# Reading the moving operands of two GEMMs in even, then odd 16-byte pieces

## The chip, the core and the metric

The kernel runs on one core of a Trainium2 chip. A core has TensorE (PE in the profile: matrix products, with weight loads listed as PEld), VectorE (DVE), ScalarE (ACT), GpSimd (POOL) and SyncE (SP), and 16 DMA engines. The metric is the device time of one launch in microseconds, lower is better. The median of three runs before the change is 673.26 us (673.08 to 673.38).

## The reference

Attention with a sliding window and four sink columns, followed by a two-layer network whose activation has a learned slope for negative values:

```python
keep = is_sink | in_window                     # 4 sinks, window of 128
scores = np.where(keep, q @ k.T / sqrt(64), -1e9)
a = softmax(scores);  attn = a @ v             # B, H, S, D = 4, 8, 768, 64
x = attn.transpose(0, 2, 1, 3).reshape(3072, 512)
h = x @ w_in                                   # 512 -> 2048
g = np.maximum(h, 0) + alpha * np.minimum(h, 0)
out = g @ w_out                                # 2048 -> 512
```

## The kernel before

The 3072 tokens are cut into 12 chunks of 256 (`QC`); a chunk lies within one batch entry. The hidden 2048 columns are cut into 16 blocks of 128, called f (`NF`). All weights are converted once, at the start, and stay in SBUF.

Products that need fp32 accuracy are made from parts in the type fp32r (four bytes, rounded, one pass of TensorE): a value is split into a high part and the rest, and three products are added: high x high, high x low and low x high. `xh` and `xl` are the parts of x, `gh` and `gl` those of g, and `fin` (called `w` in the profile) holds for one f the high and low parts of w_in and of w_out, 512 columns each.

For each chunk c and block f:

- `gemm1` (line 897) makes h for 128 hidden columns and 256 tokens. The stationary operand is 128x128 of w_in, the moving operand is 256 columns of `xh` or `xl`. There are four slices of the inner dimension (`KT`) and three products of each, so 12 matmuls of 256 columns, 2304 in all. Each has its own load of weights.
- ScalarE (L901, L903) and VectorE (L902, L904) make g, gh and gl from it.
- `gemm2` (L932, L934, L935; for the very last f of the last chunk L919 to L921) adds to the output of the chunk. The stationary operand is 128 tokens of gh or gl, the moving operand is the 512 columns of w_out's high or low part. These are six matmuls of 512 columns for each c and f, 1152 in all. It runs two f behind `gemm1` (`LAG`).

Both read the moving operand as one run of consecutive columns.

The attention of the next chunk is spread between these blocks: scores (L600, L601), softmax (L613, L617), weights times values (L789, L878, in plain fp32, 64 columns of the array at a time) and the sinks' part (L862). The end of a chunk's attention writes x: `av` for chunk 2 (L808, L811), `av_split` for chunks 0 and 1 (L844, L848), `av_four` for the others (L884, L885). Each time ScalarE writes the high part (a cast to fp32r) and VectorE the rest (a subtraction).

On L862, the moving operand is read in runs of 32 columns:

```python
nc.tensor.matmul(place(x), vt.at[:, x * P:(x + 1) * P],
                 st.at.rearrange("p (i u b) -> p u i b", u=2, i=4), start=x % 2 == 0, stop=False)
```

That makes eight runs of 32 columns (128 bytes) for 256. For the plain fp32 product of the heads' pairs 2 and 3, L878 reads its 256 moving columns in eight runs of 32 as well; L789 reads them in one run. VectorE writes runs of 32 columns on L773.

The order of instructions is not written by hand: `Plan` gives every operation a cost and draws a schedule, and each engine gets its instructions in that order. The planner's cost for a matmul is `mm(n)`, 0.456 ns a column. Short bf16 matmuls on a tile called `idle` (L1089, 512 columns) fill gaps in the first 44 us.

Behind all this stands a general version for other masks (`general`, `general_moe`). It runs only if a flag is set, which it is not with the inputs given.

On the host, w_in and w_out are laid out as one row of 512 values per partition and f; a DMA brings both for one f.

Of the kernel before, what the change touches and what calls it, by code (L numbers as in the profile page):

```python
# [19 lines left out]
P = 128  # L20
# [4 lines left out]
QC = 2 * P  # L25
# [264 lines left out]
def cast(n, psum=False):  # L290
    return (0.045 if psum else 0.092) + 0.84e-3 * n
# [27 lines left out]
ISSUE = 0.45  # L319
SINKLAG = 0.0  # L320
R_TAIL, N_TAIL, T_TAIL = 0.2, 0.65, 0.36


def program(ctx, tc, qk, pairs, vp, vq, vs, w, par, out):
# [474 lines left out]
    def av(c, p):  # L799
        src, v, bk = wt.pop((c, p)), vtile.pop((c, p)), val("pa")  # L800
        a = lambda: bk.at[:, :QC]
        vt, st = vst[c // CPB], sinkT[c]
        op("PE", mm(QC), lambda: nc.tensor.matmul(a(), vt.at[:, p * P:(p + 1) * P], st.at, start=True, stop=False),
           reads=[vt, st], writes=[bk], tail=R_TAIL)
        op("PE", values_cost(c), lambda: values(c, v.at, lambda j: src.at.bitcast(F32)[:, j * 4 * P:(j + 1) * 4 * P], a()),
           reads=[src, v], writes=[bk], tail=N_TAIL, mode="col")
        x1, x2 = begin_x(c, p)
        op("ACT", cast(QC, True), lambda: nc.scalar.copy(x1.at[:, p], a()), reads=[bk], writes=[(x1, p)])  # L808
        if p + 2 < KT:
            load_v(c, p + 2)  # L810
        op("DVE", dve(QC), lambda: nc.vector.tensor_tensor(x2.at[:, p], a(), x1.at[:, p].bitcast(F32), ALU.subtract),  # L811
           reads=[bk, (x1, p)], writes=[(x2, p)])

    def av_split(c, g):
        both = (2 * g, 2 * g + 1)
        src, v = [wt.pop((c, x)) for x in both], [vtile.pop((c, x)) for x in both]
        wide, rb = rinv[c, g], val("ob")
        rk = val("o" if c == 0 else "pa")

        def inverse():  # L820
            for n in range(2):
                for u in range(2):
                    nc.tensor.transpose(rk.at[:, (2 * n + u) * P:(2 * n + u + 1) * P],
                                        wide.at[:, (2 * u + n) * P:(2 * u + n + 1) * P], ident)
        op("PE", 4 * TURN, inverse, reads=[wide, known("ident")], writes=[rk], tail=T_TAIL)
        op("ACT", cast(4 * P, True), lambda: nc.scalar.copy(rb.at, rk.at), reads=[rk], writes=[rb])
        bk = val("pa")
        vt, st = vst[c // CPB], sinkT[c]

        def sinks():  # L830
            for n, x in enumerate(both):
                nc.tensor.matmul(bk.at[:, n * QC:(n + 1) * QC], vt.at[:, x * P:(x + 1) * P], st.at, start=n == 0, stop=False)
        op("PE", 2 * mm(QC), sinks, reads=[vt, st], writes=[bk], tail=R_TAIL)

        def both_values():
            for n in range(2):
                values(c, v[n].at, lambda j: src[n][j].at, bk.at[:, n * QC:(n + 1) * QC], n == 1)
        op("PE", 2 * values_cost(c), both_values, reads=[t for two in src for t in two] + v, writes=[bk], tail=N_TAIL, mode="col")
        x1, x2 = begin_x(c, 2 * g)
        op("DVE", dve(4 * P), lambda: nc.vector.tensor_tensor(rb.at, bk.at, rb.at, ALU.mult), reads=[bk], writes=[rb])  # L840
        view = lambda: rb.at.rearrange("p (n x) -> p n x", n=2)
        part = slice(2 * g, 2 * g + 2)
        keys = [(x1, x) for x in both], [(x2, x) for x in both]
        op("ACT", cast(4 * P), lambda: nc.scalar.copy(x1.at[:, part], view()), reads=[rb], writes=keys[0])  # L844
        if c and not g:
            for x in both:
                load_v(c, x + 2)
        op("DVE", dve(4 * P), lambda: nc.vector.tensor_tensor(x2.at[:, part], view(), x1.at[:, part].bitcast(F32), ALU.subtract),  # L848
           reads=[rb, *keys[0]], writes=keys[1])

    def av_four(c):
        every = range(KT)
        kept = [wt.pop((c, x)) for x in every]
        src = [*kept[:2], *kept[2], *kept[3]]
        v = [vtile.pop((c, x)) for x in every]
        bks = [val("pa") for _ in range(2)]
        vt, st = vst[c // CPB], sinkT[c]
        place = lambda x: bks[x // 2].at[:, x % 2 * QC:(x % 2 + 1) * QC]

        def sinks():  # L860
            for x in every:
                nc.tensor.matmul(place(x), vt.at[:, x * P:(x + 1) * P], st.at.rearrange("p (i u b) -> p u i b", u=2, i=4), start=x % 2 == 0, stop=False)  # L862
        op("PE", 4 * mm(QC), sinks, reads=[vt, st], writes=bks, tail=R_TAIL)
        x1, x2 = begin_x(c, 0)

        def all_values():
            for x in every:
                if x < 2:
                    values(c, v[x].at, lambda j: kept[x].at.bitcast(F32)[:, j * 4 * P:(j + 1) * 4 * P], place(x), x == 1)
                    continue  # L870
                t, e = kept[x]
                blocks = [(1, lambda j: t.at.rearrange("p (i j u b) -> p j u i b", i=4, j=2, u=2)[:, j], slice(0, 2 * P))]
                if c % CPB:
                    blocks.append((0, lambda j: e.at[:, j * QC:j * QC + P], slice(0, P)))
                blocks.append((2, lambda j: e.at[:, j * QC + P:(j + 1) * QC], slice(P, 2 * P)))
                for n, (blk, what, os) in enumerate(blocks):
                    for j in range(2):
                        nc.tensor.matmul(place(x)[j * D:(j + 1) * D, os], v[x].at[:, blk, j], what(j), start=False, stop=x == KT - 1 and n == len(blocks) - 1)  # L878
        op("PE", 4 * values_cost(c), all_values, reads=src + v, writes=bks, tail=N_TAIL, mode="col")
        for n, bk in enumerate(bks):  # L880
            part = slice(2 * n, 2 * n + 2)
            keys = [[(t, x) for x in range(2 * n, 2 * n + 2)] for t in (x1, x2)]
            view = lambda bk=bk: bk.at.rearrange("p (n x) -> p n x", n=2)
            op("ACT", cast(4 * P, True), lambda part=part, view=view: nc.scalar.copy(x1.at[:, part], view()), reads=[bk], writes=keys[0])  # L884
            op("DVE", dve(4 * P), lambda part=part, view=view: nc.vector.tensor_tensor(x2.at[:, part], view(), x1.at[:, part].bitcast(F32), ALU.subtract),  # L885
               reads=[bk, *keys[0]], writes=keys[1])

    gs = {}
# [1 line left out]
    def gemm1(c, f):  # L890
# [3 lines left out]
        def some(kt):  # L894
            ks = slice(kt * P, (kt + 1) * P)
            for n, (part, rhs) in enumerate(((0, x1), (0, x2), (1, x1))):
                nc.tensor.matmul(h(), fin.at[:, 0, part, ks], rhs.at[:, kt], start=(kt == 0 and n == 0), stop=(kt == KT - 1 and n == 2))  # L897
        for kt in range(KT):
            op("PE", 3 * mm(QC), lambda kt=kt: some(kt), reads=[fin, (x1, kt), (x2, kt)], writes=[bk], tail=R_TAIL)
        g, gh, gl = val("g"), val("gh"), val("gl")  # L900
# [8 lines left out]
    def gemm2(c, f, dst):  # L909
# [5 lines left out]
        if c == NCHUNK - 1 and f == NF - 1:  # L915
            for j in range(2):
                def last(j=j):
                    js = slice(j * P, (j + 1) * P)
                    nc.tensor.matmul(o2[j].at, gh.at[:, js], fin.at[:, 1, 0], start=False, stop=False)  # L919
                    nc.tensor.matmul(o2[j].at, gh.at[:, js], fin.at[:, 1, 1], start=False, stop=False)  # L920
                    nc.tensor.matmul(o2[j].at, gl.at[:, js], fin.at[:, 1, 0], start=False, stop=True)  # L921
                op("PE", 3 * mm(DM), last, reads=[fin, gh, gl], writes=[o2[j]], tail=R_TAIL)
                ob = val("ob")
                op("ACT", cast(DM, True), lambda ob=ob, j=j: nc.scalar.copy(ob.at, o2[j].at), reads=[o2[j]], writes=[ob])
# [2 lines left out]
        for lowpart in range(2):  # L927
            def some(lowpart=lowpart):
                for j in range(2):
                    js = slice(j * P, (j + 1) * P)  # L930
                    if lowpart:
                        nc.tensor.matmul(o2[j].at, gl.at[:, js], fin.at[:, 1, 0], start=False, stop=(f == NF - 1))  # L932
                    else:
                        nc.tensor.matmul(o2[j].at, gh.at[:, js], fin.at[:, 1, 0], start=(f == 0), stop=False)  # L934
                        nc.tensor.matmul(o2[j].at, gh.at[:, js], fin.at[:, 1, 1], start=False, stop=False)  # L935
            op("PE", (2 if lowpart else 4) * mm(DM), some, reads=[fin, gl if lowpart else gh], writes=o2, tail=R_TAIL)
        if f == NF - 1:
            for j in range(2):
# [184 lines left out]
def general_moe(nc, gen, ptile, f, x, wt, alt, acc):  # L1123
# [15 lines left out]
    nc.vector.tensor_tensor(gl, g, gh.bitcast(F32), ALU.subtract)  # L1139
    for j in range(2):  # L1140
        js = slice(j * P, (j + 1) * P)
        nc.tensor.matmul(acc[j], gh[:, js], wt[:, 1, 0], start=(f == 0), stop=False)
        nc.tensor.matmul(acc[j], gh[:, js], wt[:, 1, 1], start=False, stop=False)
        nc.tensor.matmul(acc[j], gl[:, js], wt[:, 1, 0], start=False, stop=(f == NF - 1))


def general_weights(nc, gen, src, dst):
# [133 lines left out]
```

## Time and profile before

| what | value |
|---|---|
| median of the runs | 673.26 us |
| the profiled execution, its own time | 673.32 us |
| its span, first to last instruction | 671.4 us |
| granted TensorE clock, mean | 0.999 |
| TensorE busy | 658.9 us, 4529 matmuls |
| weight loads busy | 577.5 us, 4529 loads |
| VectorE, ScalarE busy | 524.7 us, 397.2 us |

A row of the costliest groups reads: line, engine, operation, tile written <- tiles read, shape, count | busy time in us, mean ns of one | idle time of the engine before them and what ended it. Matmuls overlap in the pipeline, so the mean of one is longer than its share of the span. In the chain of waits a row has a start, a length and the work that filled it; `x12` are twelve instructions that follow each other. Rows by source line have the shortest, the median and the longest duration in ns.

### The profile page before, as it was taken

To read this page: it belongs to the slowest core of one execution; us is meant where nothing else is said; L and a number is where in the kernel's file an instruction comes from. 1 tells how busy PE (TensorE), PEld (TensorE's weight loads), DVE (VectorE), ACT (ScalarE), POOL (GpSimd) and SP (SyncE) were. 2 spreads that over 40 slices of the span, in tenths; PEclk is the share of its full clock that TensorE was granted. 3 is DMA by queue.
4 is the path that set the end of the run, shared out by engine and by line. 5 is a ranking of instruction groups with operands and counts; after the bars stand their busy time and mean duration, and the time that the engine had idled before them with its cause. 6 is when DMAs were issued, how large, how long until landed. Compare 5 with 4: busy or idle time off the path is not lost.

```text
span 671.4 us, 13234 instructions
## 1 busy us (share of the span) xinstructions
PE 658.9 (98%) x4529; PEld 577.5 (86%) x4529; DVE 524.7 (78%) x1750; ACT 397.2 (59%) x1066; POOL 34.5 (5%) x115
## 2 busy tenths in 40 slices
PE   8998999999999999999999999999999999999996
PEld 4577899978989989989989989988998988998985
DVE  7999999968958968976976986995995994994331
ACT  6999987737538537636736735745644753743332
POOL 2110000000000000000000000010000000000000
PEclk9999999999999999999999999999999999999999
DMA  8666542434434344443443443542542542420001
GB/s 326 217 248 236 185 165 59 116 87 147 132 103 143 114 124 123 133 140 87 144 122 101 143 127 96 160 120 73 167 133 70 163 138 80 143 95 17 32 2 35
DMA packets 58683, 84.67 MB, mean 126 GB/s; under 512 B 9072, under 2 KB 35056, under 8 KB 58608
## 3 DMA queue, kind: packets, MB, share of 16 engines
q1 hardware_dynamic: 55056, 70.64, 34.4%
q10 hardware_dynamic: 3552, 13.11, 5.4%
q8 instruction: 37, 0.61, 0.4%
q14 instruction: 38, 0.31, 0.1%
HBM read 66.69 MB, written 17.04 MB: 125 GB/s over the span
## 4 chain that ended last, share of the span: by engine, by line
PE 83%; DVE 11%; ACT 2%; issue 1%; POOL 0%; DMA 0%; ACTq 0%; DVEq 0%
PE bank L897 36%; PE bank L934 12%; PE bank L932 12%; PE bank L935 12%; PE bank L789 3%; PE bank L600 3%; PE bank L601 3%; PE bank L878 2%; DVE wa L398 2%; DVE w L406 2%; DVE wa L396 1%; DVE wa L389 1%; DVE pt L613 1%; ACT pt L617 1%; DVE gl L904 1%
## 5 line engine op out<-in xcount | busy, mean ns | idle before, releaser
L897 PE MATMUL bank<-xh,w 128*128 128x256 f32 x1536 | 306.5, 282 | 1.2 <-DVE g L902 1.2
L897 PEld LDWEIGHTS bank<-xh,w 128*128 128x128 f32 x1536 | 249.6, 189 | 9.9 <-DVE g L902 3.8
L897 PE MATMUL bank<-xl,w 128*128 128x256 f32 x768 | 214.3, 279 | 0.0
L901 ACT ACTIVATE g<-bank,param 128x256 f32<-128x256 f32 x192 | 90.6, 473 | 115.3 <-PE bank L897 110.8
L934 PE MATMUL bank<-w,gh 128*128 128x512 f32 x382 | 151.4, 396 | 0.5 <-ACT gh L903 0.5
L935 PE MATMUL bank<-w,gh 128*128 128x512 f32 x382 | 150.0, 393 | 0.0
L897 PEld LDWEIGHTS bank<-xl,w 128*128 128x128 f32 x768 | 144.5, 188 | 4.3
L617 ACT ACTIVATE pt<-pt,nm 128x260 f32<-128x260 f32 (+1 forms) x192 | 94.5, 493 | 50.7 <-DVE nm L613 50.4
L902 DVE TENSOR_TENSOR g<-bank,g 128x256 f32<-128x256 f32 x192 | 79.6, 419 | 51.8 <-ACT g L901 51.4
L932 PE MATMUL bank<-w,gl 128*128 128x512 f32 x382 | 119.7, 395 | 0.0
L903 ACT CAST gh<-g 128x256 fp32r<-128x256 f32 x192 | 76.9, 404 | 61.2 <-DVE g L902 61.1
L904 DVE TENSOR_TENSOR gl<-g,gh 128x256 fp32r<-128x256 f32 x192 | 80.2, 422 | 25.3 <-ACT gh L903 22.2
L613 DVE CUSTOM_DVE_ANT_0 pt<-bank,masks 128x260 f32<-128x260 f32 (+1 forms) x192 | 75.0, 401 | 14.9 <-PE bank L601 13.7
L932 PEld LDWEIGHTS bank<-w,gl 128*128 128x128 f32 x382 | 70.5, 188 | 16.1 <-issue 0.9
L934 PEld LDWEIGHTS bank<-w,gh 128*128 128x128 f32 x382 | 71.8, 188 | 9.1 <-ACT gh L903 0.8
L935 PEld LDWEIGHTS bank<-w,gh 128*128 128x128 f32 x382 | 71.8, 188 | 8.3
L566 DVE TENSOR_TENSOR kq<-stage,kq 64x392 fp32r<-64x392 f32 x80 | 45.2, 565 | 3.0 <-ACT kq L564 0.4
L662 POOL TENSOR_TENSOR sink<-pt,ri 128x8 f32<-128x8 f32 x80 | 19.8, 251 | 504.4 <-DVE ri L647 358.6
L601 PE MATMUL bank<-kq 128*128 128x260 f32 (+1 forms) x160 | 45.0, 281 | 0.0
L600 PE MATMUL bank<-kq 128*128 128x260 f32 (+1 forms) x160 | 44.7, 280 | 0.1
L658 DVE CUSTOM_DVE_ANT_0 comb<-pt,ri 128x128 f32<-128x128 f32 x136 | 43.1, 343 | 0.4
L564 ACT CAST kq<-stage 128x392 fp32r<-128x392 f32 x80 | 41.0, 512 | 2.5 <-PE bank L601 2.2
(131 smaller groups left out, 680.8 us busy)
## 6 DMA issues: line engine op xcount, KB each, us to landing
stage<-qk SPq DMA_DIRECT2D x80, 324.0 KB, 2.9
wraw<-w ACTq DMA_DIRECT2D x12, 1024.0 KB, 5.1
swap<-comb SPq DMA_DIRECT2D x36, 256.0 KB, 2.0
comb<-swap SPq DMA_DIRECT2D x36, 256.0 KB, 3.0
v<-vq SPq DMA_DIRECT2D x36, 192.0 KB, 2.5
out_dram<-ob SPq DMA_DIRECT2D x22, 256.0 KB, 3.5
wraw<-w SPq DMA_DIRECT2D x4, 1024.0 KB, 8.7
v<-vp SPq DMA_DIRECT2D x8, 192.0 KB, 8.1
```

Source lines behind the costliest of these rows:

```text
L600: nc.tensor.matmul(s[:, w0], qh()[:, qs], ks()[:, kw], start=True, stop=False)
L601: nc.tensor.matmul(s[:, w0], ql()[:, qs], ks()[:, kw], start=False, stop=True)
L613: op("DVE", dve(n), lambda: nc.vector.tensor_tensor_reduce(out=pt.at[:, u, w0], in0=s.at[:, w0], in1=masks[:, i, w0], scale=-0.125, scalar ...
L617: op("ACT", exp(n), lambda: nc.scalar.activation(pt.at[:, u, w0], pt.at[:, u, w0], AF.Exp, bias=nm.at[:, h, u:u + 1], scale=-1.0, accum_ou ...
L897: nc.tensor.matmul(h(), fin.at[:, 0, part, ks], rhs.at[:, kt], start=(kt == 0 and n == 0), stop=(kt == KT - 1 and n == 2))
L901: op("ACT", act(QC, True), lambda: nc.scalar.activation(g.at, h(), AF.Copy, scale=alt[:, f:f + 1]), reads=[bk, known("param")], writes=[g])
L902: op("DVE", dve(QC), lambda: nc.vector.tensor_tensor(g.at, h(), g.at, ALU.max), reads=[bk], writes=[g])
L903: op("ACT", cast(QC), lambda: nc.scalar.copy(gh.at, g.at), reads=[g], writes=[gh])
L904: op("DVE", dve(QC), lambda: nc.vector.tensor_tensor(gl.at, g.at, gh.at.bitcast(F32), ALU.subtract), reads=[g, gh], writes=[gl])
L932: nc.tensor.matmul(o2[j].at, gl.at[:, js], fin.at[:, 1, 0], start=False, stop=(f == NF - 1))
L934: nc.tensor.matmul(o2[j].at, gh.at[:, js], fin.at[:, 1, 0], start=(f == 0), stop=False)
L935: nc.tensor.matmul(o2[j].at, gh.at[:, js], fin.at[:, 1, 1], start=False, stop=False)
```

## The change

x and w_out are stored with their columns in another order. Take the pieces of four fp32 values (16 bytes) of a row in memory: the even pieces hold the first half of the columns, in order, and the odd pieces the second half. The matmuls of both GEMMs read their moving operand through a view that goes over all even pieces and then over all odd ones. So they take the columns in the same logical order as before, and outputs, stationary operands and sums are unchanged. For 256 columns these are 64 runs of four columns, for 512 they are 128.

x is written in that order by ScalarE and VectorE (their output, and the high part that the subtraction reads, go through the same view); w_out gets it on the host, before the launch. The general version reads w_out through the view too.

```diff
+def in_turn(a):
+    return a.rearrange("p (l t e) -> p t l e", t=2, e=4)
+def as_is(a):
+    return a.rearrange("p (t l e) -> p t l e", t=2, e=4)
...
 # av
-nc.scalar.copy(x1.at[:, p], a())
+nc.scalar.copy(in_turn(x1.at[:, p]), as_is(a()))
-nc.vector.tensor_tensor(x2.at[:, p], a(), x1.at[:, p].bitcast(F32), ALU.subtract)
+nc.vector.tensor_tensor(in_turn(x2.at[:, p]), as_is(a()), in_turn(x1.at[:, p].bitcast(F32)), ALU.subtract)
...
 # av_split; av_four in the same way, from the bank
-view = lambda: rb.at.rearrange("p (n x) -> p n x", n=2)
+view = lambda: rb.at.rearrange("p (n t l e) -> p t n l e", n=2, t=2, e=4)
+turned_ = lambda x: x.at[:, part].rearrange("p n (l t e) -> p t n l e", t=2, e=4)
-nc.scalar.copy(x1.at[:, part], view())
+nc.scalar.copy(turned_(x1), view())
-nc.vector.tensor_tensor(x2.at[:, part], view(), x1.at[:, part].bitcast(F32), ALU.subtract)
+nc.vector.tensor_tensor(turned_(x2), view(), turned_(x1).bitcast(F32), ALU.subtract)
...
 # gemm1
-nc.tensor.matmul(h(), fin.at[:, 0, part, ks], rhs.at[:, kt], ...)
+nc.tensor.matmul(h(), fin.at[:, 0, part, ks], in_turn(rhs.at[:, kt]), ...)
...
 # gemm2, all nine calls of the two GEMM2 forms and of general_moe
-nc.tensor.matmul(o2[j].at, gh.at[:, js], fin.at[:, 1, 0], ...)
+nc.tensor.matmul(o2[j].at, gh.at[:, js], in_turn(fin.at[:, 1, 0]), ...)
...
 # host
-w[:, 1] = inputs['moe_w_out'].reshape(NF, P, DM)
+w[:, 1] = inputs['moe_w_out'].reshape(NF, P, 2, DM // 8, 4).swapaxes(2, 3).reshape(NF, P, DM)
```

More of the change, by code (lines that the diff above doesn't have):

```diff
@@ L807, in av @@
         x1, x2 = begin_x(c, p)
-        op("ACT", cast(QC, True), lambda: nc.scalar.copy(x1.at[:, p], a()), reads=[bk], writes=[(x1, p)])
+        op("ACT", cast(QC, True), lambda: nc.scalar.copy(in_turn(x1.at[:, p]), as_is(a())), reads=[bk], writes=[(x1, p)])
         if p + 2 < KT:
             load_v(c, p + 2)
-        op("DVE", dve(QC), lambda: nc.vector.tensor_tensor(x2.at[:, p], a(), x1.at[:, p].bitcast(F32), ALU.subtract),
+        op("DVE", dve(QC), lambda: nc.vector.tensor_tensor(in_turn(x2.at[:, p]), as_is(a()), in_turn(x1.at[:, p].bitcast(F32)), ALU.subtract),
            reads=[bk, (x1, p)], writes=[(x2, p)])
@@ L840, in av_split @@
         op("DVE", dve(4 * P), lambda: nc.vector.tensor_tensor(rb.at, bk.at, rb.at, ALU.mult), reads=[bk], writes=[rb])
-        view = lambda: rb.at.rearrange("p (n x) -> p n x", n=2)
+        view = lambda: rb.at.rearrange("p (n t l e) -> p t n l e", n=2, t=2, e=4)
+        turned_ = lambda x: x.at[:, part].rearrange("p n (l t e) -> p t n l e", t=2, e=4)
         part = slice(2 * g, 2 * g + 2)
         keys = [(x1, x) for x in both], [(x2, x) for x in both]
-        op("ACT", cast(4 * P), lambda: nc.scalar.copy(x1.at[:, part], view()), reads=[rb], writes=keys[0])
+        op("ACT", cast(4 * P), lambda: nc.scalar.copy(turned_(x1), view()), reads=[rb], writes=keys[0])
         if c and not g:
@@ L847, in av_split @@
                 load_v(c, x + 2)
-        op("DVE", dve(4 * P), lambda: nc.vector.tensor_tensor(x2.at[:, part], view(), x1.at[:, part].bitcast(F32), ALU.subtract),
+        op("DVE", dve(4 * P), lambda: nc.vector.tensor_tensor(turned_(x2), view(), turned_(x1).bitcast(F32), ALU.subtract),
            reads=[rb, *keys[0]], writes=keys[1])
@@ L882, in av_four @@
             keys = [[(t, x) for x in range(2 * n, 2 * n + 2)] for t in (x1, x2)]
-            view = lambda bk=bk: bk.at.rearrange("p (n x) -> p n x", n=2)
-            op("ACT", cast(4 * P, True), lambda part=part, view=view: nc.scalar.copy(x1.at[:, part], view()), reads=[bk], writes=keys[0])
-            op("DVE", dve(4 * P), lambda part=part, view=view: nc.vector.tensor_tensor(x2.at[:, part], view(), x1.at[:, part].bitcast(F32), ALU.subtract),
+            view = lambda bk=bk: bk.at.rearrange("p (n t l e) -> p t n l e", n=2, t=2, e=4)
+            turned_ = lambda x, part=part: x.at[:, part].rearrange("p n (l t e) -> p t n l e", t=2, e=4)
+            op("ACT", cast(4 * P, True), lambda turned_=turned_, view=view: nc.scalar.copy(turned_(x1), view()), reads=[bk], writes=keys[0])
+            op("DVE", dve(4 * P), lambda turned_=turned_, view=view: nc.vector.tensor_tensor(turned_(x2), view(), turned_(x1).bitcast(F32), ALU.subtract),
                reads=[bk, *keys[0]], writes=keys[1])
@@ L896, in some @@
             for n, (part, rhs) in enumerate(((0, x1), (0, x2), (1, x1))):
-                nc.tensor.matmul(h(), fin.at[:, 0, part, ks], rhs.at[:, kt], start=(kt == 0 and n == 0), stop=(kt == KT - 1 and n == 2))
+                nc.tensor.matmul(h(), fin.at[:, 0, part, ks], in_turn(rhs.at[:, kt]), start=(kt == 0 and n == 0), stop=(kt == KT - 1 and n == 2))
         for kt in range(KT):
@@ L918, in last @@
                     js = slice(j * P, (j + 1) * P)
-                    nc.tensor.matmul(o2[j].at, gh.at[:, js], fin.at[:, 1, 0], start=False, stop=False)
-                    nc.tensor.matmul(o2[j].at, gh.at[:, js], fin.at[:, 1, 1], start=False, stop=False)
-                    nc.tensor.matmul(o2[j].at, gl.at[:, js], fin.at[:, 1, 0], start=False, stop=True)
+                    nc.tensor.matmul(o2[j].at, gh.at[:, js], in_turn(fin.at[:, 1, 0]), start=False, stop=False)
+                    nc.tensor.matmul(o2[j].at, gh.at[:, js], in_turn(fin.at[:, 1, 1]), start=False, stop=False)
+                    nc.tensor.matmul(o2[j].at, gl.at[:, js], in_turn(fin.at[:, 1, 0]), start=False, stop=True)
                 op("PE", 3 * mm(DM), last, reads=[fin, gh, gl], writes=[o2[j]], tail=R_TAIL)
@@ L931, in some @@
                     if lowpart:
-                        nc.tensor.matmul(o2[j].at, gl.at[:, js], fin.at[:, 1, 0], start=False, stop=(f == NF - 1))
+                        nc.tensor.matmul(o2[j].at, gl.at[:, js], in_turn(fin.at[:, 1, 0]), start=False, stop=(f == NF - 1))
                     else:
-                        nc.tensor.matmul(o2[j].at, gh.at[:, js], fin.at[:, 1, 0], start=(f == 0), stop=False)
-                        nc.tensor.matmul(o2[j].at, gh.at[:, js], fin.at[:, 1, 1], start=False, stop=False)
+                        nc.tensor.matmul(o2[j].at, gh.at[:, js], in_turn(fin.at[:, 1, 0]), start=(f == 0), stop=False)
+                        nc.tensor.matmul(o2[j].at, gh.at[:, js], in_turn(fin.at[:, 1, 1]), start=False, stop=False)
             op("PE", (2 if lowpart else 4) * mm(DM), some, reads=[fin, gl if lowpart else gh], writes=o2, tail=R_TAIL)
@@ L1141, in general_moe @@
         js = slice(j * P, (j + 1) * P)
-        nc.tensor.matmul(acc[j], gh[:, js], wt[:, 1, 0], start=(f == 0), stop=False)
-        nc.tensor.matmul(acc[j], gh[:, js], wt[:, 1, 1], start=False, stop=False)
-        nc.tensor.matmul(acc[j], gl[:, js], wt[:, 1, 0], start=False, stop=(f == NF - 1))
+        nc.tensor.matmul(acc[j], gh[:, js], in_turn(wt[:, 1, 0]), start=(f == 0), stop=False)
+        nc.tensor.matmul(acc[j], gh[:, js], in_turn(wt[:, 1, 1]), start=False, stop=False)
+        nc.tensor.matmul(acc[j], gl[:, js], in_turn(wt[:, 1, 0]), start=False, stop=(f == NF - 1))
 def general_weights(nc, gen, src, dst):
```

## The prediction, made before the changed kernel was run

> **What bounds the kernel now.** I read the page from the top: share of busy time, granted clock, the chain that ended last, then the costliest groups.
>
> ```profile
> span 671.4 us, 13234 instructions
> PE 658.9 (98%) x4529; PEld 577.5 (86%) x4529; DVE 524.7 (78%) x1750; ACT 397.2 (59%) x1066; POOL 34.5 (5%) x115
> PEclk9999999999999999999999999999999999999999
> PE 83%; DVE 11%; ACT 2%; issue 1%; POOL 0%; DMA 0%; ACTq 0%; DVEq 0%
> L897 PE MATMUL bank<-xh,w 128*128 128x256 f32 x1536 | 306.5, 282 | 1.2 <-DVE g L902 1.2
> L897 PE MATMUL bank<-xl,w 128*128 128x256 f32 x768 | 214.3, 279 | 0.0
> L934 PE MATMUL bank<-w,gh 128*128 128x512 f32 x382 | 151.4, 396 | 0.5 <-ACT gh L903 0.5
> L935 PE MATMUL bank<-w,gh 128*128 128x512 f32 x382 | 150.0, 393 | 0.0
> L932 PE MATMUL bank<-w,gl 128*128 128x512 f32 x382 | 119.7, 395 | 0.0
> ```
>
> TensorE works 98% of the span at its full clock, and nothing in the two GEMMs waits for another engine: the idle time before these groups is about a microsecond in all. What one matmul of them lasts is the kernel's time, one for one. The durations (282, 396 ns) overlap, since matmuls are pipelined; what counts is the distance from one start to the next. It comes from the chain of waits between 100 and 640 us, where that chain is TensorE's alone:
>
> ```profile
> by line: PE bank L897 42.3%; PE bank L934 14.0%; PE bank L932 13.9%; PE bank L935 13.9%; PE bank L789 3.7%; PE bank L600 3.5%; PE bank L601 3.4%; PE bank L878 2.7%; PE bank L862 0.8%; PE bank L731 0.3%; DVE w L406 0.2%; DVE wa L398 0.2%; PE
> ```
>
> That stretch has 1,967 matmuls on L897 and 983 on L932 to L935 (counts below). So one of 256 columns takes 0.423 x 540 us / 1967 = 116.1 ns of the chain, and one of 512 columns 0.418 x 540 / 983 = 229.6 ns. Groups of twelve on L897 in the same chain (start, length) are of two kinds:
>
> ```profile
> 263.82 1.36 PE bank L897 x12
> ...
> 267.06 1.41 PE bank L897 x12
> ...
> 273.08 1.42 PE bank L897 x12
> ...
> 279.64 1.36 PE bank L897 x12
> ```
>
> Same work, same shapes, 113.3 or 118 ns a matmul. The durations by line (shortest/median/longest, ns) show the same spread, and then what a matmul lasts while no weights are loaded:
>
> ```profile
> L897 PE MATMUL bank<-xh,w x1311: 276/280/388, 99.9 to 638.8; 128*128 128x256 f32 x188
> L897 PE MATMUL bank<-xl,w x656: 276/280/287, 99.8 to 638.7; 128*128 128x256 f32 x164
> L932 PE MATMUL bank<-w,gl x327: 388/392/505, 102.0 to 639.8; 128*128 128x512 f32 x164
> L934 PE MATMUL bank<-w,gh x328: 388/396/481, 101.1 to 639.4; 128*128 128x512 f32 x164
> L935 PE MATMUL bank<-w,gh x328: 388/393/403, 101.3 to 639.6; 128*128 128x512 f32 x164
> L932 PE MATMUL bank<-w,gl x1: 388/388/388, 549.7 to 549.7; 128*128 128x512 f32 x1
> 549.46 0.19 PEld L932 LDWEIGHTS bank<-w,gl 128*128 128x128 f32 x1
> 549.98 0.19 PEld L897 LDWEIGHTS bank<-xh,w 128*128 128x128 f32 x1 [0.32 <-DVE g L902]
> L1089 PE MATMUL bank<-idle x12: 379/379/382, 19.4 to 32.9; 128*128 128x512 bf16 x12
> ```
>
> The matmul that starts at 549.7 has no weight load beside it (the next starts at 549.98) and lasts the minimum, 388 ns. With one, 512 columns last up to 403 ns and 256 columns 276 to 287. So I read two losses: a variable one, when weight load and moving operand are read together (mean 394.4 - 388 = 6.4 ns on the three GEMM2 lines, 116.1 - 113.3 = 2.8 ns on L897), and a constant one, 388 against 379 ns for a bf16 matmul of the same width: 9 ns per 512 columns.
>
> **The change part by part.** Matmuls, weight loads, columns and bytes stay as they are; the 4529 records of each kind should return.
>
> 1. The reading order of the moving operand, in 2304 matmuls on L897 and 1152 on L919 to L935 (3 x 382 and 6). It is unpriced: no row reads in runs of four columns. The lowest bound by rows is that both losses go: 1152 x (6.4 + 9) + 2304 x (2.8 + 4.5) = 17.7 + 16.8 = 34.5 us less (4.5 is half of 9, an estimate). The highest comes from the one fp32r matmul with a broken reading order, the sinks' product on L862, in eight runs of 32 columns:
>
> ```profile
> L862 PE MATMUL bank<-sinkT,vs x36: 278/283/286, 186.4 to 605.9; 128*128 128x256 f32 x36
> L789 PE MATMUL bank<-wa,v 128*64 128x256 f32 x88 | 13.9, 394 | 0.0
> L878 PE MATMUL bank<-comb,v 128*64 128x256 f32 x72 | 10.8, 379 | 0.0
> ```
>
> Its median is 3 ns above L897's: 0.43 ns for each of seven joins between runs. Against that, the plain fp32 products show no price of a join: L878 reads eight runs of 32 and lasts 379 ns, L789 reads 256 in one run and lasts 394. [...] With 63 joins per 256 and 127 per 512 columns there are 291,456 joins; at 0.43 ns that is 125 us more.
>
> Between the two I take the variable loss as gone and the constant one as kept. The row nearest to the edit is L897's own: one address pattern, one shape, and yet whole groups lock into 1.36 or into 1.41 us. So the loss hangs on how two regular streams fall on each other, and the change alters just that: the moving stream keeps to even pieces for half its columns, while the load goes through all of them. After a first collision has shifted one against the other, I expect them to stay apart, as in the 1.36 us groups. Gain: 2304 x 2.8 = 6.4 and 1152 x 6.4 = 7.3, together 13.7 us.
>
> The Trainium skill speaks against this in "SBUF — State Buffer", section "Who interferes with whom": TensorE has two independent read ports, and it never waits on anyone. By that a load costs the matmul nothing and this term would be 0 us, the sum 673.3. The rows above (388 without a load, a mean of 394.4 with it) disagree, and I go by them.
>
> 2. Writing x in pieces: L884/L885, L844/L848, L808/L811.
>
> ```profile
> L884 ACT CAST xh<-bank 128x512 fp32r<-128x512 f32 x18 | 10.6, 587 | 25.0 <-PE bank L789 15.9 <-PE bank L878 9.0
> L885 DVE TENSOR_TENSOR xl<-bank,xh 128x512 fp32r<-128x512 f32 x18 | 12.5, 692 | 25.5 <-ACT xh L884 25.5
> L844 ACT CAST xh<-ob 128x512 fp32r<-128x512 f32 x4 | 2.4, 612 | 0.0
> L848 DVE TENSOR_TENSOR xl<-ob,xh 128x512 fp32r<-128x512 f32 x4 | 2.7, 683 | 0.0
> L773 DVE TENSOR_TENSOR wa<-comb,tri 128x256 f32<-128x256 f32 x72 | 27.2, 406 | 0.0
> L904 DVE TENSOR_TENSOR gl<-g,gh 128x256 fp32r<-128x256 f32 x192 | 80.2, 422 | 25.3 <-ACT gh L903 22.2 <-PE bank L1051 0.5
> 561.64 0.69 DVE L885 TENSOR_TENSOR xl<-bank,xh 128x512 fp32r<-128x512 f32 x1 [1.04 <-ACT xh L884]
> 565.50 0.28 PE L897 MATMUL bank<-xh,w 128*128 128x256 f32 x1
> ```
>
> L773 handles runs of 32 in 406 ns, L904 one run of 256 in 422: broken order costs VectorE nothing there. I take 0 us. If each of these took twice as long, the cover is the time from the last xl (ends 561.64 + 0.69 = 562.33) to its first use at 565.50: 3.2 us, against 2 x (0.59 + 0.69) = 2.6 us more. Uncovered is only the start, where chunks 0 and 1 feed TensorE directly: 2 x (0.612 + 0.683) = 2.6 us for one chunk's two pairs, the upper bound. Behind a longer L884 on ScalarE stand L901 and L903 of the next f; GEMM2 runs two f behind them.
>
> 3. w_out is permuted on the host. Its transfer stays one row of the same length, and the conversions (L384 to L406) work element by element: 0 us, either side, since no instruction, byte count or order of theirs changes.
>
> 4. `general_moe` doesn't run with these inputs (no row of its lines): 0 us.
>
> Sum: the profiled execution took 673.32 us (671.4 us of span and 1.9 around it), 0.06 from the median of 673.26. 673.3 - 13.7 = 659.6 us.
>
> **The rivals.**
>
> *Both losses go.* The constant 9 ns might also come from the order in which consecutive pieces are read. For it: it grows with fp32r and is absent in bf16, so it hangs on bytes per column. Against: it stands unmoved in every state, at 276 and 388. Price -34.5 us: 638.8 us.
>
> *Nothing moves.* The pieces are still whole ones, each read in four columns. The Trainium skill has such a rule ("SBUF — State Buffer", section "Specifications (TRN2)": lines of 16 bytes, a penalty for crossing to a new one); by it the crossings are equally many and the time stays. As a mechanism of this kernel: 64 and 128 pieces per matmul before and after, and the phases mix as now, half the groups at 1.36 and half at 1.41. 673.3 us. Against it: the chain's groups react to phase, so an exact tie needs a coincidence.
>
> *Slower by collisions.* While the moving stream stays on even pieces, every second piece of the load meets it on the same side, for the whole load; there is no phase to lock into. Then each matmul lasts its longest, 287 instead of 280 ns on L897 and 403 instead of 394.4 on GEMM2: 2304 x 7 + 1152 x 8.6 = 26 us, 699.3 us. It decides as soon as L897's mean start distance passes 116.1 ns. For it: L862, whose order is broken, never reaches 276 and lasts 283. Against: L862's longest, 286, stays within L897's.
>
> *Slower by joins.* Each join has a price of its own. At 0.43 ns: 673.3 + 125 = 798 us. From 0.047 ns a join (13.7 us / 291,456) on, the forecast's gain is eaten. For it: L862's shortest, 278, lies above 276. Against: L878.
>
> **How the numbers follow.** The forecast's case gets 0.34, both losses gone 0.13, nothing 0.12, collisions 0.24, joins 0.17. L862 is the sole near row for joins, and its 3 ns may be collisions as well, so joins stay below collisions. A change under 0.2% (1.3 us) can't be told from none in this kernel. Faster: 0.34 + 0.13 = 0.47; same 0.12; slower 0.24 + 0.17 = 0.41. The range runs from the second case (638.8, less 2.6 for its rounded terms) to the collisions' case with the uncovered x at the start and some joins (699.3 + 2.6 + 4): 636 to 706, which leaves the joins out. The likeliest case alone: 653 to 667, that is half to one and a half times its gain.
>
> **What would show it.** Right: the two kinds of groups on L897 become one at about 1.36 us; medians of 276 and 388 ns; L884 and L885 near 587 and 692 ns; TensorE still at 98%. Both losses gone: shortest durations under 276 and 388. Collisions: medians near 287 and 403, with a matmul that has no load beside it still at 388. Joins: that matmul longer too, by the same per column in all lines. Wrong altogether, if idle time appears before L897 with ACT xh or DVE xl as its releaser.

## The result and the profile after

The changed kernel takes 678.14 us (median of 4, 677.75 to 679.57) against 673.27 us: ratio 1.0076, 95% interval 1.0059 to 1.0094. It is slower by 4.9 us; 659.6 us was forecast. The profiled execution took 679.57 us, 1.4 above its median: in one slice of its page the clock was granted at 8 tenths, which the kernel before doesn't show there, so single times of it are read with 1 to 2 us in mind.

The page after, the same rows as before (L908 is the first GEMM, L943 to L946 the second):

```profile
span 677.6 us, 13234 instructions
...
PE 666.2 (98%) x4529; PEld 582.3 (86%) x4529; DVE 525.6 (78%) x1750; ACT 399.0 (59%) x1066; POOL 34.6 (5%) x115
...
PEclk9998999999999999999999999999999999999999
...
L908 PE MATMUL bank<-xh,w 128*128 128x256 f32 x1536 | 310.2, 283 | 1.1 <-DVE g L913 1.1
...
L908 PE MATMUL bank<-xl,w 128*128 128x256 f32 x768 | 215.5, 281 | 0.0
```

Count and shapes are the same, TensorE is as busy as before, and still next to nothing waits for another engine. Each matmul takes a little longer. In the chain of waits, the prediction read the groups of twelve on the first GEMM (start, length) as two kinds, 1.36 and 1.41 us. After, the stretch from 262 to 284 us has seven of them, 1.41 or 1.42 us each. Four of these:

```profile
263.32 1.41 PE bank L908 x12
266.61 1.41 PE bank L908 x12
269.88 1.41 PE bank L908 x12
272.93 1.42 PE bank L908 x12
```

They became nearly one kind, as the prediction's test asked, but the long one. From the starts of all whole groups between 100 and 640 us: after, 115 of 143 last 1.41 or 1.42 us and the others longer. Before, 63 of 144 lasted 1.36 to 1.39 us, 51 lasted 1.40 to 1.42, and 30 longer; there were more kinds than two. The durations by line (shortest/median/longest, ns), and last a wide matmul that has no weight load beside it:

```profile
L908 PE MATMUL bank<-xh,w x1299: 277/280/386, 99.8 to 639.2; 128*128 128x256 f32 x186
L943 PE MATMUL bank<-w,gl x324: 391/394/501, 101.2 to 637.6; 128*128 128x512 f32 x162
L945 PE MATMUL bank<-w,gh x326: 392/395/478, 100.2 to 639.8; 128*128 128x512 f32 x163
L946 PE MATMUL bank<-w,gh x326: 392/393/399, 100.5 to 640.0; 128*128 128x512 f32 x163
L943 PE MATMUL bank<-w,gl x1: 391/391/391, 554.8 to 554.8; 128*128 128x512 f32 x1
```

The weight loads around that last one (start, length):

```profile
554.34 0.42 PEld L943 LDWEIGHTS bank<-w,gl 128*128 128x128 f32 x2
555.07 0.19 PEld L908 LDWEIGHTS bank<-xh,w 128*128 128x128 f32 x1 [0.32 <-DVE g L913]
```

The shortest durations rose, 276 to 277 and 388 to 391 ns. The matmul without a load beside it (it starts at 554.8, the next load at 555.07) went from 388 to 391 as well, but one such matmul says little. Between 100 and 640 us each trace has eight wide ones with no load in their first 230 ns: before, six last 388 ns and two 392 and 393; after, five last 391 and three 394. The longest plain ones (403 on L935 before, 399 on L946) fell. So the floor went up and the spread went down.

How much it is: from the starts of matmuls that follow each other, leaving out those behind which TensorE waited (over 130 and 245 ns), the mean distance is 116.2 ns before and 117.9 after on the first GEMM (2238 and 2242 of them), 231.2 and 232.7 on the second (1125 each). 2304 x 1.8 + 1152 x 1.4 = 5.7 us (an estimate), and 4.9 were measured.

The writing of x shows no price (rows of ScalarE and VectorE after; 587 and 692 ns before). Only the four casts of chunks 0 and 1 went from 612 to 626 ns, 0.06 us in all.

```profile
L895 ACT CAST xh<-bank 128x512 fp32r<-128x512 f32 x18 | 10.6, 587 | 26.0 <-PE bank L798 17.0 <-PE bank L888 9.0
L896 DVE TENSOR_TENSOR xl<-bank,xh 128x512 fp32r<-128x512 f32 x18 | 12.5, 692 | 26.5 <-ACT xh L895 26.5
```

### The profile page after: what moved, and what is told of

Its sections match the earlier page's. It is cut to its first block, busy times and chain, and to the rows that moved or that the text cites. A ratio compares the mean times of both kernels' runs of the same rounds, so it can differ in the third digit from the quotient of the medians.

```text
span 677.6 us, 13234 instructions
## 1 busy us (share of the span) xinstructions
PE 666.2 (98%) x4529; PEld 582.3 (86%) x4529; DVE 525.6 (78%) x1750; ACT 399.0 (59%) x1066; POOL 34.6 (5%) x115
## 4 chain that ended last, share of the span: by engine, by line
PE 89%; DVE 7%; ACT 2%; issue 1%; POOL 0%; DMA 0%; ACTq 0%; DVEq 0%
PE bank L908 39%; PE bank L943 13%; PE bank L945 13%; PE bank L946 13%; PE bank L798 3%; PE bank L610 3%; PE bank L609 3%; PE bank L888 2%; DVE wa L407 1%; DVE w L415 1%; DVE wa L398 1%; DVE pt L622 1%; PE bank L872 1%; ACT pt L626 1%; ACT wa L393 0%
## 5 line engine op out<-in xcount | busy, mean ns | idle before, releaser
L908 PE MATMUL bank<-xh,w 128*128 128x256 f32 x1536 | 310.2, 283 | 1.1 <-DVE g L913 1.1
L908 PEld LDWEIGHTS bank<-xh,w 128*128 128x128 f32 x1536 | 249.9, 188 | 10.1 <-DVE g L913 3.6
L908 PE MATMUL bank<-xl,w 128*128 128x256 f32 x768 | 215.5, 281 | 0.0
L946 PE MATMUL bank<-w,gh 128*128 128x512 f32 x382 | 150.4, 394 | 0.0
L908 PEld LDWEIGHTS bank<-xl,w 128*128 128x128 f32 x768 | 144.4, 188 | 4.3
L943 PE MATMUL bank<-w,gl 128*128 128x512 f32 x382 | 120.4, 396 | 0.0
L943 PEld LDWEIGHTS bank<-w,gl 128*128 128x128 f32 x382 | 70.4, 188 | 16.5 <-issue 0.5
L946 PEld LDWEIGHTS bank<-w,gh 128*128 128x128 f32 x382 | 71.9, 188 | 8.6
```

The source lines that it names most:

```text
L908: nc.tensor.matmul(h(), fin.at[:, 0, part, ks], in_turn(rhs.at[:, kt]), start=(kt == 0 and n == 0), stop=(kt == KT - 1 and n == 2))
L943: nc.tensor.matmul(o2[j].at, gl.at[:, js], in_turn(fin.at[:, 1, 0]), start=False, stop=(f == NF - 1))
L946: nc.tensor.matmul(o2[j].at, gh.at[:, js], in_turn(fin.at[:, 1, 1]), start=False, stop=False)
```

## The experiments

Ratios are against the kernel before on the same chip.

**One GEMM at a time.** `e1` keeps the change for x alone, `e2` for w_out alone:

```diff
 # e1: gemm2, general_moe and the host layout as before; one line of each kind is shown
-nc.tensor.matmul(o2[j].at, gh.at[:, js], in_turn(fin.at[:, 1, 0]), ...)
+nc.tensor.matmul(o2[j].at, gh.at[:, js], fin.at[:, 1, 0], ...)
 # e2: gemm1 and the writing of x as before
-nc.tensor.matmul(h(), fin.at[:, 0, part, ks], in_turn(rhs.at[:, kt]), ...)
+nc.tensor.matmul(h(), fin.at[:, 0, part, ks], rhs.at[:, kt], ...)
```

> Only x is stored and read in even, then odd pieces; w_out is read as one run, as before. In the changed kernel's trace a 256-column matmul on the first GEMM starts 117.9 ns after the one before it, against 116.2 before, and without a weight load beside it lasts 278 instead of 276 ns. Theory A (the new reading order costs each matmul a constant amount of its own): 2304 x 1.8 = +4.1 us, ratio 1.006, and shortest durations of 278 ns on the first GEMM and 388 on the second. Theory B (the added time is collisions with weight loads, whose phase runs on from one GEMM to the other): the two halves don't add up; this one gives anything between -3 and +8 us, and the second GEMM's lines change as well.

> Only w_out is stored and read in even, then odd pieces; x as before. In the changed kernel's trace a 512-column matmul starts 232.7 ns after the one before, against 231.2, and without a load beside it lasts 391 instead of 388 ns. Theory A: 1152 x 1.4 = +1.6 us, ratio 1.0025, shortest duration of 391 ns on the second GEMM and 276 on the first. Theory B: not additive with the other half, between -3 and +5 us.

Measured: x alone 677.55 us, ratio 1.0062 (1.0049 to 1.0076); w_out alone 674.19 us, 1.0012 (1.0003 to 1.0021). The two add up to 1.0074; both together gave 1.0076. That speaks for A, though w_out alone stays below A's 1.0025. Most of the loss is x's. With w_out alone the first GEMM keeps its 276 ns and the second has the raised floor:

```profile
L906 PE MATMUL bank<-xh,w x1312: 276/278/388, 99.7 to 639.7; 128*128 128x256 f32 x188
L941 PE MATMUL bank<-w,gl x326: 391/394/501, 102.0 to 638.2; 128*128 128x512 f32 x163
```

A did not hit everything: in `e1`, the first GEMM starts every 117.9 ns as A said, but the second moved from 231.2 to 232.1 without an edit to it, and in `e2` the first fell from 116.2 to 115.7. So each GEMM's spacing also depends on the other's, which is what B said of the phase; the runs don't rule out that some of the added time is of that kind.

**The reading orders by themselves.** `e3` and `e5` add groups of equal matmuls behind the end of the kernel before, 32 or 40 in a row, with one line for each group:

```diff
+def turn(a, t, e):
+    return a.rearrange("p (l t e) -> p t l e", t=t, e=e)
 # M(o, n), W(o, n): n columns from column o of two converted weight tiles
 # one such line per order, width and load:
+plan.emit(lambda: [nc.tensor.matmul(hb[0:1, :256], W(0, 1), turn(M(16, 256), 2, 4), start=True, stop=True) for _ in range(32)])
```

> The kernel before with 1280 matmuls more behind its end, in groups of 32 that each repeat one reading order, with a stationary operand of 1 column (next to no load) or of 128. Their results are thrown away. Theory A: with 1 column, 256 columns in even-odd pieces last 2 ns more than in one run (278 against 276) and 512 columns 3 ns more; if it is a price of a join, it grows with the number of runs (4x4, 2x4, 2x8, 2x16, 2x32 have 64, 64, 32, 16 and 8 runs), if it is one jump a matmul, all orders cost alike. Theory B: with 1 column all orders with whole pieces last the same, and they differ only with 128. Where single columns are taken with a step of two or pieces of two columns (2x1, 2x2), each piece of memory is touched twice as often: up to double the time if a piece costs two steps. The two scans move the start of the moving operand by 16 bytes against the load's: if the variable loss (113.3 against 118 ns) is a collision of two regular streams, the start distances in them spread from 113 to 123 ns and from 226 to 240, the same for all 32 of a group but the first few; if the offset doesn't matter, all sixteen groups show one value for each width.

In `e3`, L1100 to L1107 have a load of 1 column, which takes 82 ns instead of 188 and so is little, but not none; their orders (t x e: turns by columns in a run) are one run, 2x4, 4x4, 2x8, 2x16, 2x32, 2x2 and 2x1. L1108 to L1110 have a load of 128 columns and the orders one run, 2x4 and 4x4. Loads and matmuls by duration, for the two loads and for the first three orders:

```profile
L1100 PEld LDWEIGHTS bank<-w,w x32: 81/82/83, 665.3 to 669.0; 128*1 128x1 f32 x32
L1100 PE MATMUL bank<-w,w x32: 276/276/280, 665.6 to 669.1; 128*1 128x256 f32 x32
L1101 PE MATMUL bank<-w,w x32: 277/279/280, 669.2 to 672.8; 128*1 128x256 f32 x32
L1102 PE MATMUL bank<-w,w x32: 270/271/277, 672.9 to 676.4; 128*1 128x256 f32 x32
L1108 PEld LDWEIGHTS bank<-w,w x32: 187/188/211, 702.5 to 706.3; 128*128 128x128 f32 x32
```

The chain of `e3` (start, length of 32 matmuls):

```profile
665.74 3.65 PE bank L1100 x32
669.38 3.72 PE bank L1101 x32
673.10 3.53 PE bank L1102 x32
676.63 3.70 PE bank L1103 x32
680.33 3.90 PE bank L1104 x32
684.22 3.78 PE bank L1105 x32
688.00 7.46 PE bank L1106 x32
695.47 7.47 PE bank L1107 x32
702.94 3.77 PE bank L1108 x32
706.70 3.84 PE bank L1109 x32
710.54 3.72 PE bank L1110 x32
```

Leaving out the first eight of each group, which still settle, the mean start distances with 1 column are 113.3 ns for one run, 116.3 for even-odd (2x4), 110.0 for 4x4, 115.6 for 2x8, 121.8 for 2x16 and 118.2 for 2x32. With 128 columns it is 117.8, 120.0 and 115.7 for the first three. All of these have one start of the moving operand against the load, 64 bytes on. Four things follow for it:

- The order of pieces has a price that needs no wide weight load: +3.0 ns for even-odd on 256 columns, and -3.3 ns for 4x4.
- It is not a price of joins: 4x4 has 64 runs, as many as 2x4, and is the shortest; 2x16 has 16 and is the longest of whole pieces.
- The wide load adds to these three orders: 4.5 ns to one run, 3.7 to even-odd, 5.7 to 4x4. Changing the moving order does not take it away.
- A piece read only by half (2x2, 2x1) costs double, 233 ns. The Trainium skill ("SBUF — State Buffer", section "Specifications (TRN2)") asks for two hits in a line of 16 bytes for full bandwidth; for these fp32r matmuls the runs show that two hits aren't enough.

For 512 columns, the groups don't settle the size: with 1 column 231.6 ns in one run and 230.7 even-odd, with 128 columns 233.2 and 233.5. A's 3 ns don't show there; the small price of `e2` is carried by the kernels alone.

In the two scans, one run of 256 columns settles at 113.35 ns when the moving operand starts 64 or 112 bytes after the load and between 116.7 and 120.0 otherwise; 512 columns range from 226.65 (start 0) to 233.4 (96). The spread lies inside the expected one, though not every group settles at one value. Two cautions follow. With the wide load, the start alone moves one run by 6.7 ns, and at two starts of eight no price of the load is left; the 2.2 ns between one run and even-odd lie inside that spread, so there the price of the order rests on the kernels. And L1108 has the relative start 64 as well but takes 117.8 ns: the scan's group differs from it in that both streams begin 96 bytes further on, and in what ran before it. The relative start alone doesn't set the value.

**More steps, and four turns in the kernel.** In `e4`, the changed kernel has t=4 instead of t=2, in the views and on the host:

```diff
-    return a.rearrange("p (l t e) -> p t l e", t=2, e=4)
+    return a.rearrange("p (l t e) -> p t l e", t=4, e=4)
...
-    w[:, 1] = inputs['moe_w_out'].reshape(NF, P, 2, DM // 8, 4).swapaxes(2, 3).reshape(NF, P, DM)
+    w[:, 1] = inputs['moe_w_out'].reshape(NF, P, 4, DM // 16, 4).swapaxes(2, 3).reshape(NF, P, DM)
```

> The changed kernel with four turns instead of two: every fourth piece of 16 bytes first, then those behind them, for x and w_out. Joins: as many as with two turns. In the groups of repeated matmuls, 256 columns in that order start 110.0 ns apart with a stationary operand of 1 column (113.3 in one run, 116.3 even-odd), and 115.7 with 128 columns (117.8 in one run, 120.0 even-odd). Theory A' (the order of pieces sets a loss of the moving stream's own, joins and writing cost nothing): about 2 ns less than before on each of 2304 matmuls and up to twice that on the 1152 wide ones, -5 to -10 us against before, ratio 0.985 to 0.993, and shortest durations under 276 and 388 ns. Rival (any order in pieces costs the kernel the same, since joins or the writing of x have the price): ratio 1.005 to 1.010 as with two turns.

> The kernel before with groups of 40 repeated matmuls behind its end, results thrown away: steps of 1, 2, 4, 8, 16, 32 and 64 pieces between the pieces read one after another (t x 4), runs of 8 and 16 columns, both widths, and 4x4 at four starts against the load's. Theory A': the start distance depends on the step between pieces and not on the number of joins; 4x4 stays the shortest at 110 ns with 1 column, 4x8 (half the joins) is not between 4x4 and one run. A single memory of pieces that follow each other in turn would make large steps (8, 16, 32) either all equal to 4x4 or all slow (twice the time, as for half pieces); joins would make all t x 4 of one width equal.

`e4` takes 666.84 us, ratio 0.9908 (0.9894 to 0.9922): faster than both kernels, with one digit changed against the slower one. Its rows by line:

```profile
L908 PE MATMUL bank<-xh,w x1327: 270/275/389, 99.9 to 639.9; 128*128 128x256 f32 x190
L943 PE MATMUL bank<-w,gl x332: 378/382/489, 101.6 to 639.5; 128*128 128x512 f32 x166
L945 PE MATMUL bank<-w,gh x332: 378/383/469, 100.7 to 638.8; 128*128 128x512 f32 x166
```

The floor follows the order of pieces: 276, 277 and 270 ns on the first GEMM, 388, 391 and 378 on the second, for one run, two turns and four. With four turns it reaches the 379 ns of a bf16 matmul of that width. The number of joins, the bytes and the writing of x (587 and 692 ns) are those of two turns; the rival is out.

The chain of `e5` (40 matmuls each): 256 columns with a load of 1 column and the orders 8x4, 16x4, 32x4 and 64x4, the last of which is one run again; then 512 columns with a load of 128 in one run, 2x4, 4x4, 8x4 and 16x4:

```profile
709.39 4.70 PE bank L1109 x40
714.10 5.34 PE bank L1110 x40
719.44 4.99 PE bank L1111 x40
724.43 4.54 PE bank L1112 x40
...
733.54 9.34 PE bank L1114 x40
742.88 9.33 PE bank L1115 x40
752.22 9.06 PE bank L1116 x40
761.28 9.95 PE bank L1117 x40
771.22 11.10 PE bank L1118 x40
```

The price depends on the step between pieces and in no even way: by the same mean, steps of 8, 16 and 32 pieces give 116.9, 133.6 and 124.4 ns, against 113.3, 116.3 and 110.0 for steps of 1, 2 and 4. On 512 columns it is 233.3, 233.2, 226.5, 249.1 and 277.7 for steps of 1, 2, 4, 8 and 16. Neither simple picture (all large steps alike, or all at double) holds; what makes these steps so different stays open. Runs of eight columns with a step of four (4x8) have half the joins of 4x4 and take 114.0 ns, more than 4x4 and more than one run: again no price of joins. With the wide load, 4x4 takes 113.7 to 116.8 ns by its start.

**Moving the starts.** `e6` is `e4`, `e7` the kernel before, with x and g's parts placed elsewhere against the loads:

```diff
-several("xh", 2, [P, KT, QC], F32R)
-several("xl", 2, [P, KT, QC], F32R)
+for n_ in ("xh", "xl"):
+    plan.kind(n_, [pool.tile([P, KT * QC + 32], F32R, name=f"{n_}{i}")[:, 12:12 + KT * QC].rearrange("p (k q) -> p k q", k=KT) for i in range(2)])
 several("g", 2, [P, QC], F32)
+pool.tile([P, 8], F32, name="pad")    # e7: 16
```

> Four turns, with x starting 48 bytes further on against the weight loads (relative start 112 instead of 64 bytes, modulo 128) and gh, gl 32 bytes further on. Theory C (the part of the loss that comes with a load is set by where the two streams start against each other): by the groups of repeated matmuls 113.7 instead of 116.4 ns on 256 columns and 225.3 instead of 226.5 on 512, so -4 to -7 us against four turns alone, about 661 us, ratio 0.981 to 0.985. Rival (in the kernel the phase comes from what ran before, and the start does not matter): as four turns alone, 667 us, ratio 0.991.

> The kernel before, read in one run, with x starting 48 bytes further on (relative start 112 instead of 64) and gh, gl 64 bytes further on (relative start 0 instead of 64). In the groups of repeated matmuls these starts settled at 113.35 ns for 256 and 226.65 ns for 512 columns, all alike. Theory C: 116.2 becomes 113.4 and 231.2 becomes 226.7: 2304 x 2.8 + 1152 x 4.5 = 11.6 us less, about 661.6 us, ratio 0.983. Rival (the phase is inherited, and relative start 64, which the kernel has now, settled at 113.35 ns in such a group as well, yet the kernel shows 113 and 118): within 2 us of 673.3, ratio 0.997 to 1.003.

Measured: `e6` 667.64 us, ratio 0.9922 (0.9908 to 0.9935), as four turns alone; `e7` 675.87 us, 1.0042 (1.0028 to 1.0056). Theory C falls with `e7`: starts that settled in a group of equal matmuls at 113.35 ns gave 117.3 ns in the kernel. (`e6` is the weaker test: its price for x, 113.7 ns, is that of a group at 48 bytes, while x starts at 112.) The rival, within 2 us, missed as well. In the kernel, a group of twelve alternates between xh and xl and takes other weights each time, and it begins where the matmuls before it left off. The placing matters (2.7 us in `e7`), but the groups don't foretell its sign. What sets the long and the short groups in the kernel is not settled.

These traces also show what a wide matmul without a load beside it is worth as a measure. In `e7`, which reads in one run as the kernel before, all eight of them last 397 or 398 ns; in `e1`, where w_out is read in one run too, six of eight do. In `e4` nine of ten last 390 or 391, far above that kernel's shortest of 378. One such matmul of `e7`, the loads around it, and one of `e4`:

```profile
L933 PE MATMUL bank<-w,gl x1: 398/398/398, 551.3 to 551.3; 128*128 128x512 f32 x1
551.06 0.19 PEld L933 LDWEIGHTS bank<-w,gl 128*128 128x128 f32 x1
551.60 0.19 PEld L898 LDWEIGHTS bank<-xh,w 128*128 128x128 f32 x1 [0.36 <-DVE g L903]
L943 PE MATMUL bank<-w,gl x1: 391/391/391, 544.3 to 544.3; 128*128 128x512 f32 x1
```

So a wide matmul can lose ten nanoseconds with no load beside it: the varying part of its duration is not the load's alone. The shortest durations, on the other hand, go by the order of pieces in all nine kernels, wherever the operands start: 275 or 276 and 387 or 388 ns in one run, 277 and 391 with two turns, 270 and 377 or 378 with four.

**Four turns, planned anew and for w_out alone.**

```diff
 # e8: e4 with
 def mm(n):
-    return 0.456e-3 * n
+    return 0.443e-3 * n
 # e9: e2 with t=4, e=4 and the host layout of e4
```

> Four turns with the planner's cost of a matmul lowered from 0.456 to 0.443 ns a column, near what the four-turn kernel shows (115.1 ns for 256 and 224.4 for 512 columns). The four-turn kernel lost part of its gain to waits: per matmul it should have gained 2304 x 1.1 + 1152 x 6.8 = 10.3 us and gained 6.4. If the schedule is what gives that back (TensorE arrives before ScalarE and VectorE), a plan drawn for the new pace brings 1 to 4 us: 663 to 666 us, ratio 0.985 to 0.989. Rival (the waits come from the engines themselves): 0.990 to 0.993.

> Four turns for w_out alone, x in one run. Theory A' (the order of pieces sets a loss of each matmul's own, so the two GEMMs add up): 1152 x 6.8 = 7.8 us less at the most, some of it given back in waits, 666 to 669 us, ratio 0.989 to 0.994; the first GEMM stays at 116.2 ns. Rival (the gain comes from both streams keeping the same order): ratio over 0.996.

`e9` takes 667.43 us, ratio 0.9914 (0.9902 to 0.9927). Nearly the whole gain of four turns is w_out's: 231.2 to 224.2 ns a matmul, 1152 x 7.0 = 8.1 us (an estimate), of which 5.8 arrive by the ratio; the first GEMM has 115.8. `e8` missed: 677.65 us, 1.0054 (1.0034 to 1.0074). Its matmuls are as short as those of `e4` (115.0 and 224.3 ns), but TensorE now waits before the first GEMM, 10.2 us between 100 and 640 us, where there were 0.7 us in the kernel before:

```profile
L908 PE MATMUL bank<-xh,w 128*128 128x256 f32 x1288 | 255.0, 280 | 10.2 <-DVE g L913 10.2
```

A price nearer to the measured pace made a worse plan here. Not all of the 677.65 us is the plan's: five of the six executions were granted a clock of 0.992 or 0.993, against 0.996 to 0.999 for the kernel before, and the one with 0.999 took 674.49 us, still no gain. In `e4` and `e9` TensorE is idle for 1.9 and 1.7 us between 100 and 640 us, 0.8 in the kernel before, so waits give back about 1 us and are not shown to be the whole of what is missing. That this plan repairs it is refuted.

## Why the prediction was wrong

The direction and the size were wrong. The time lies inside the range, but that range (636 to 706) was wide enough for both directions; "slower" had 0.41.

- **The bound** was right: what one matmul of the GEMMs lasts is the kernel's time. The change moved nothing else, and 5.7 us worked out from start distances stand against 4.9.
- **The step that failed** is the choice in step 1, "the variable loss as gone and the constant one as kept". The constant loss was not kept: the shortest durations went from 276 to 277 and from 388 to 391 ns, and they follow the order of pieces in all nine kernels. The variable loss did not go: on the first GEMM no group of twelve below 1.41 us was left, and on the second the mean duration less the shortest fell only from 6.4 to 4.2 ns (395.2 - 391). The term of 2304 x 2.8 + 1152 x 6.4 = 13.7 us less became 2304 x 1.8 + 1152 x 1.4 = 5.7 us more. How these divide between an order's own price (+3.0 ns on 256 columns in the groups) and the phase is not shown.
- **The reading under it**, that the variable loss comes "when weight load and moving operand are read together", was shown on one matmul of 388 ns. The same trace has two without a load beside them of 392 and 393, the first of which is shown here, and `e7`, in the same order, has eight of 397 or 398:

```profile
L935 PE MATMUL bank<-w,gh x1: 392/392/392, 349.0 to 349.0; 128*128 128x512 f32 x1
348.74 0.19 PEld L935 LDWEIGHTS bank<-w,gh 128*128 128x128 f32 x1
349.29 0.20 PEld L789 LDWEIGHTS bank<-wa,v 128*64 128x64 f32 x4 [0.37 <-issue]
```

- **The reason given for it** was that after a first collision the two streams stay apart. Most groups of twelve did become alike, but at 1.41 us. That the 1.36 and 1.41 us groups came from one address pattern showed that phase matters; it did not show that this edit would choose the good phase.
- **Against "both losses go"** the prediction held that the constant loss "stands unmoved in every state, at 276 and 388". But every state of that trace had the same reading order. A number that never varies in a trace in which its cause never varies says nothing of that cause. With four turns it does move, to 270 and 378.
- **"Slower by collisions"** had the right sign, and its own condition, a mean start distance above 116.1 ns, was met with 117.9. Its size was not: it asked for medians of 287 and 403 and 26 us more; the medians are 280 and 393 to 395. Its second test, a matmul without a load still at 388, decides nothing, since such matmuls last 388 to 398 ns in one and the same order. That every group takes the long kind is in part what this rival says; it is not ruled out as a share of the 1.8 ns.
- **"Slower by joins"** is refuted: four turns have the same joins and are faster than one run. L862's 283 ns, its only support, was no price of its order: with the same code the line has 280 after (L872):

```profile
L872 PE MATMUL bank<-sinkT,vs x36: 277/280/287, 188.5 to 611.4; 128*128 128x256 f32 x36
```

- **"Nothing moves"** failed by 4.8 us in time and clearly in mechanism: equally many pieces, crossed equally often, last differently by the step between them.
- **Steps 2 to 4** were right at 0 us: 587 and 692 ns stayed to the digit. The independent ports of the Trainium skill ("SBUF — State Buffer", section "Who interferes with whom") don't hold for time here: in the groups at one start, a load of 128 columns instead of 1 adds 3.7 to 5.7 ns to the matmul beside it. At two of the scan's eight starts it adds nothing (113.35 ns).

What stays open is why steps of 2, 8 and 16 pieces cost and a step of 4 gains, and what picks the phase.

## What to carry to other kernels

When TensorE is busy all the time, compare the shortest duration of a matmul with that of another type at the same width: the gap, here 388 against 379 ns, is a loss of the reading itself and can depend on the order in which 16-byte pieces are read. Such an order is to be scanned with a stationary operand of one column and then tried in the kernel, since neighbours in the scan differ in sign (two turns +0.8%, four turns -0.9%). One matmul without a load is no measure of the reading's own loss; the shortest of many is steadier. A phase that is seen to lock is no reason to expect the good lock from an edit, and a scan of equal matmuls did not foretell it.

## What the runs showed of the hardware

- In groups of equal ones at one start, an fp32r matmul of 256 columns starts every 110.0 ns with a step of four 16-byte pieces, 113.3 in one run, 116.3 with a step of two, 133.6 with a step of sixteen (load of 1 column).
- Pieces read by halves double the time: 233.4 ns for 256 columns. Even-odd runs of four columns that begin 8 bytes off a piece do as well, 228.0 ns, while one run begun there takes 117.7.
- With four turns an fp32r matmul of 512 columns lasts 378 ns at the shortest in the kernel, no longer than the bf16 one with 379.
- An fp32r matmul of 512 columns in one run lasts 388 to 398 ns with no weight load beside it, by kernel and place.
